# Two decode attentions on one core: all engines' programs rolled into loops over the 16 groups of heads, and a head's maximum taken with a 32x32 transpose on VectorE

## The chip, the core and the metric

The kernel runs on one core of a Trainium2 chip. The metric is the device time of one launch in microseconds (us). TensorE (PE) multiplies matrices, VectorE (DVE) does elementwise work and reductions, ScalarE (ACT) does exponentials and copies, GpSimd (POOL) sets constants, and SyncE (SP) issues nearly all DMA transfers. SBUF holds 128 partitions; PSUM holds the results of matmuls. Each engine runs its own instruction stream and meets the others only at semaphores.

## The reference

The same computation is done twice, for A and for B, with other data. One query token attends to a cache of 8192 keys and values in each of 32 heads of 128 elements; all of it is bf16.

```python
q      = (x @ wq).reshape(1, 1, 32, 128).transpose(0, 2, 1, 3)      # x: 1x1x512, wq: 512x4096
scores = einsum("bhqd,bhkd->bhqk", q, k_cache) * 128 ** -0.5        # k_cache: 1x32x8192x128
p      = softmax(scores, axis=-1)
o      = einsum("bhqk,bhkd->bhqd", p, v_cache)                      # v_cache: 1x32x8192x128
y      = o.transpose(0, 2, 1, 3).reshape(1, 1, 4096) @ wo           # wo: 4096x512
# result: concatenate([y of A, y of B], axis=-1), 1x1x1024
```

Both caches of A and B and the four weights are 285 MB, and each byte is read once.

## The kernel before

**Tiling.** The 64 heads are taken in `NM = 16` groups of `G = 4`; group n is 0 to 7 for A and 8 to 15 for B. A head has 32 partitions, so partition `h*32 + p` holds keys `p*256` to `p*256 + 255` of the group's head h. The keys of a group, called K(n) here, are one transfer of 8192 KB into `kn`, which has two buffers, used in turn; the values V(n) are one transfer of 8192 KB into `vn`, which has one buffer. `vn` first holds both `wq`, and `kn`'s first buffer holds both `wo` at the end.

**A group's work.** K(n) is handled in four chunks c of 64 keys per partition.

- `plan_mul` (L351): DVE multiplies the chunk in place by the broadcast query, 128x8192 elements.
- `plan_red` (L357): PE sums groups of 8 of the 128 products into PSUM `rps`, by 16 matmuls of 512 columns with the identity as weights. Two PSUM slots are used in turn.
- `plan_sr` (L373): DVE sums the last 8, which gives 64 scores per partition in `s_sb`.
- `plan_max` and `plan_gmax` (L379 to L388): DVE takes each partition's maximum `m1`; PE transposes it with an fp32 matmul; DVE takes the maximum of each head's 32 partitions.
- `plan_exp` (L398 to L410): PE spreads the four maxima over the partitions, ACT negates and scales them, and then does four exponentials, one for each head, which also sum.
- `plan_sum` (L415), `plan_pv` (L433): PE sums the sums over partitions, and multiplies the probabilities `pt` with V(n) in 64 matmuls, four at a time in four strips of PSUM `acc`.
- `plan_acc` (L451), `plan_turn` (L459), `plan_o` (L465): ACT copies `acc` out, PE turns it, and DVE divides into `oD`.

**Order.** The values of group n are multiplied a group late. In round n, PE does `red(n,0)`, `red(n,1)`, `red(n,2)`, then `sum(n-1)` and `pv(n-1)`, then `red(n,3)` and `turn(n-1)`. DVE does `mul` 0, 1, `sr` 0, `mul` 2, `sr` 1, `mul` 3, `sr` 2, `sr` 3, the maximum, `o(n-1)`, and the head's maximum. In round 0 there is no `pv`; there the query projection of B, `plan_q(1, 0)` and `plan_q(1, 1)`, stands ahead of `red(0,3)`. The query projection of A stands ahead of all rounds. A `plan_q(a, j)` is 16 matmuls with 32 columns of weights each, four at a time in four strips of `qyp`, and one ACT copy (L339).

**Programs.** `_Plan` records every operation and the waits that it needs, one list for each engine. PE's list is emitted as a loop over rounds 1 to 15 (`_Loop`, `emit_pe`), with one copy of the 16 matmuls for each buffer of `kn` and every address fixed. DVE's is a loop over pairs of rounds. ACT's is written out in full. SP's list is straight code.

**SP's list**, in order: `wq` of A, the two `x`, K(0), `wq` of B, K(1), V(0), K(2), V(1), K(3) and so on to V(14), `wo` of A and half of `wo` of B, V(15) in two pieces, the rest of `wo` of B in five pieces. SP issues one after the other, and each waits as follows:

```python
load_k(n):  red_done[n - 2, 3]      # the buffer's last reduction; K(1) waits only for x
load_v(n):  pv_done[n - 1]          # V(0): q_done[1], the last projection matmul of B
```

**Output projection.** `wo` rows are multiplied with `oD`, spread over partitions (`plan_relayout`, `plan_wo` L528 and L533: four strips at a time); the last 16 heads of B use L572, as their `wo` pieces land.

Of the kernel before, what the change touches and what calls it, by code (L numbers as in the profile page):

```python
# [5 lines left out]
AF = mybir.ActivationFunctionType  # L6
# [6 lines left out]


class _Ctr:


    def __init__(self, nc, stack, name):
        self.sem = stack.enter_context(nc.semaphore(name))
        self.n = 0  # L20
        self.name = name


class _Plan:


    def __init__(self):
        self.prog = {"SP": [], "PE": [], "ACT": [], "DVE": [], "POOL": []}
        self.waited = {}

    def wait(self, eng, mark):
        if mark is None:
            return
        ctr, val = mark
        if val <= 0 or self.waited.get((eng, ctr.name), 0) >= val:
            return
        self.waited[(eng, ctr.name)] = val
        self.prog[eng].append((None, ctr, val))

    def op(self, eng, fn, ctr=None, needs=(), inc=1):  # L40

        for m in needs:
            self.wait(eng, m)
        self.prog[eng].append((fn, ctr, inc))
        if ctr is None:
            return None
        ctr.n += inc
        return ctr, ctr.n


def _emit(e, items, slot=None):
    for fn, ctr, k in items:
        if fn is None:
            e.wait_ge(ctr.sem, k)
        elif isinstance(fn, tuple):
            which, fns = fn
            if slot is None:
                fns[which](e).then_inc(ctr.sem, k)
            else:
                with e.If_eq(slot, 0):  # L60
                    fns[0](e).then_inc(ctr.sem, k)
                with e.Else():
                    fns[1](e).then_inc(ctr.sem, k)
        elif ctr is None:
            fn(e)
        else:
            fn(e).then_inc(ctr.sem, k)


def _steps(items):  # L70


    out, waits = [], []
    for it in items:
        if it[0] is None:
            waits.append(it[1:])
        else:
            out.append((waits, it))
            waits = []
    assert not waits  # L80
    return out


class _Loop:


    def __init__(self, e, rounds):
        self.e = e
        rounds = [_steps(r) for r in rounds]
        assert len({len(r) for r in rounds}) == 1  # L90
        early, self.body, self.last = [], [], []
        for k in range(len(rounds[0])):
            at = [r[k] for r in rounds]
            assert all(it[1:] == at[0][1][1:] for _, it in at)
            first, second, third = at[0][0], at[1][0], at[2][0]
            waits = []
            for (ctr, v), (_, w) in zip(second, third):
                d = w - v
                assert v - d >= 1
                waits.append((ctr, v - d, d))  # L100
            for n, (ws, _) in enumerate(at[1:], 1):
                assert [(c, v) for c, v in ws] == [(c, v + n * d) for c, v, d in waits]
            for ctr, v in first:
                same = [x for c, x, _ in waits if c is ctr]
                if not same:
                    early.append((None, ctr, v))
                else:
                    assert v <= same[0]
            self.body.append((waits, at[0][1]))
            self.last.append([(c, v + len(rounds) * d) for c, v, d in waits])  # L110
        self.early = early
        self.regs = {}
        for k, (waits, _) in enumerate(self.body):
            for i, (ctr, v, d) in enumerate(waits):
                if d:
                    self.regs[k, i] = e.alloc_register("w%d_%d" % (k, i))
                    e.reg_mov(self.regs[k, i], v)

    def emit(self, k, slot):
        e = self.e  # L120
        waits, it = self.body[k]
        for i, (ctr, v, d) in enumerate(waits):
            e.wait_ge(ctr.sem, self.regs.get((k, i), v))
        _emit(e, [it], slot)
        for i, (ctr, v, d) in enumerate(waits):
            if d:
                e.reg_add(self.regs[k, i], self.regs[k, i], d)


def bass_concat_heads__mha_block_cached__gqa_block_cached__decode_kernel(  # L130
# [32 lines left out]
    NK = 2  # L163
# [6 lines left out]
    assert Dh % DW == 0  # L170

    WOG = [[(0, 32)], [(0, 16), (16, 8), (24, 4), (28, 2), (30, 1), (31, 1)]]
    BEFORE = 1
    HT = [32, 16]
    RG = [32, 16, 8, 4, 2]
    VLAST = (0, T - CT, T)

    with ExitStack() as st:
        ec = st.enter_context

        def sb(name, shape, dt):
            return ec(nc.sbuf_tensor(name, shape, dt))

        kn = sb("kn", [P, NK, T, Dh], BF16)
        vn = sb("vn", [P, T, Dh], BF16)

        def flat(ap):
            return ap.rearrange("p t d -> p (t d)")

        W = C * H * Dh  # L190
        assert T * Dh == NA * W
# [37 lines left out]
        def ps(name, shape):  # L229
            return ec(nc.psum_tensor(name, shape, F32))  # L230
# [532 lines left out]
```

## Time and profile before

| what | value |
|---|---|
| time, median of 3 runs | 666.33 us (666.32 to 666.51) |
| the profiled execution's own time | 666.81 us |
| its span, first to last instruction | 665.6 us |
| mean TensorE clock granted | 0.796 |
| PE busy | 377.9 us, 57% |
| DVE busy | 341.2 us, 51% |
| ACT busy | 71.8 us, 11% |
| DMA | 285.31 MB, 429 GB/s over the span |

The times below count from the span's start, so the execution's own time is 1.2 us longer than the span. In a row of the timeline stand start, duration, engine, source line, operation, written tile, read tiles, shape, count, and in brackets how long the engine had been idle and what released it. SPq is SP issuing a transfer. Durations of "x2" and more are from the first start to the last end.

### The profile page before, as it was taken

The numbers are of one execution on the slowest core, as the hardware profiler recorded it, in microseconds if no ns is written. First come the engines' busy times: TensorE is split into PE (matmuls) and PEld (weight loads), VectorE is DVE, ScalarE is ACT, GpSimd is POOL, SyncE is SP. The second block draws the span as 40 slices with busy tenths as digits, with TensorE's granted clock in tenths as the row PEclk, the third lists the DMA queues.
The fourth block names the chain that finished last, engine by engine and source line by source line (L and its number), as shares of the span: only waits on it lengthen the run. The fifth ranks groups of instructions, "written<-read, shape, count | busy, mean of one in ns | idle before, by whom it ended". The sixth has DMA issues, their size and how long they took to land.

```text
span 665.6 us, 6342 instructions
## 1 busy us (share of the span) xinstructions
PE 377.9 (57%) x2569; PEld 176.0 (26%) x2569; DVE 341.2 (51%) x220; ACT 71.8 (11%) x167; POOL 3.0 (0%) x15
## 2 busy tenths in 40 slices
PE   1165755828285582828557281845738184573854
PEld 0022332403132241313224131322413132231422
DVE  1095817456281845638184563818456380835630
ACT  1002020010202011020201002020100202020020
POOL 1000000000000000000000000000000000000000
PEclk9998886959687695968779596877959687795987
DMA  9999999999999999999999999999999999999997
GB/s 380 435 447 434 434 438 437 410 429 441 437 437 437 437 437 418 421 441 441 433 437 437 441 425 410 441 441 433 437 437 441 433 410 433 441 437 433 412 437 302
DMA packets 6069, 285.31 MB, mean 429 GB/s; under 512 B 683, under 2 KB 942, under 8 KB 1198
## 3 DMA queue, kind: packets, MB, share of 16 engines
q1 hardware_dynamic: 6056, 285.22, 99.3%
q8 instruction: 4, 0.07, 0.0%
q14 instruction: 3, 0.02, 0.0%
q10 hardware_dynamic: 6, 0.00, 0.0%
HBM read 285.21 MB, written 0.00 MB: 429 GB/s over the span
## 4 chain that ended last, share of the span: by engine, by line
DMA 40%; PE 29%; DVE 15%; another core or an unknown queue 13%; issue 2%; SPq 0%; DVEq 0%; ACT 0%
PE rps L362 20%; DMA vn<-in_A_v_cache_dram 16%; DVE kn L353 13%; DMA vn<-in_B_v_cache_dram 10%; PE acc L433 8%; DMA kn<-in_A_k_cache_dram 7%; DMA kn<-in_B_wo_dram 5%; DMA kn<-in_B_x_dram 2%; DVE s_sb L373 1%; DVE m L379 1%; PE mtp L385 1%; SPq L256 0%; PE misc L415 0%; ACT xb L317 0%
## 5 line engine op out<-in xcount | busy, mean ns | idle before, releaser
L362 PE MATMUL rps<-kn,ident 128*128 128x512 bf16 x1024 | 265.6, 422 | 242.4 <-DVE kn L353 242.4
L353 DVE TENSOR_TENSOR kn<-kn,qbc 128x8192 bf16<-128x8192 bf16 x64 | 281.5, 4419 | 169.1 <-DMA kn<-in_A_k_cache_dram 89.2
L362 PEld LDWEIGHTS rps<-kn,ident 128*128 128x128 bf16 x1024 | 105.2, 107 | 396.2 <-issue 305.4
L373 DVE TENSOR_REDUCE s_sb<-rps 128x64 f32<-128x512 f32 x64 | 44.0, 688 | 118.0 <-PE rps L362 118.0
L433 PE MATMUL acc<-vn,pt 128*16 128x512 bf16 x1024 | 59.7, 386 | 10.9 <-DMA vn<-in_B_v_cache_dram 10.2
L451 ACT COPY xb<-acc 128x512 f32<-128x512 f32 x16 | 9.4, 585 | 438.6 <-PE acc L433 438.6
L410 ACT ACTIVATE pt<-s_sb,negb 32x256 bf16<-32x256 f32 x64 | 54.8, 857 | 1.9
L433 PEld LDWEIGHTS acc<-vn,pt 128*16 128x16 bf16 x1024 | 24.3, 91 | 39.0 <-DMA vn<-in_B_v_cache_dram 9.6
L398 PE MATMUL bmp<-gm,hrow 1*128 1x1 f32 x128 | 17.8, 256 | 6.0 <-DVE gm L388 6.0
L398 PEld LDWEIGHTS bmp<-gm,hrow 1*128 1x128 f32 x128 | 16.5, 197 | 10.7 <-DVE gm L388 10.0
L459 PEld LDWEIGHTS bmp<-tsel,xb 128*128 128x128 f32 x128 | 16.7, 191 | 3.3 <-ACT xb L451 1.2
L410 ACT ACTIVATION_READ_ACCUMULATOR pt<-s_sb,negb 32x1 f32 x64 | 15.9, 248 | 0.0
L459 PE MATMUL bmp<-tsel,xb 128*128 128x4 f32 x128 | 15.3, 243 | 0.7 <-ACT xb L451 0.7
L402 ACT ACTIVATE negb<-bmp 128x1 f32<-128x1 f32 x16 | 2.7, 171 | 97.1 <-PE bmp L398 97.1
L465 DVE TENSOR_TENSOR oD<-bmp,rinv 128x4 f32 (+1 forms) x16 | 2.4, 153 | 16.6 <-PE bmp L459 16.6
L385 PE MATMUL mtp<-ident_f,m 128*1 128x128 f32 x32 | 6.1, 270 | 8.0 <-DVE m L379 8.0
L313 PE MATMUL misc<-ones_bf,kn 1*128 1x128 bf16 x4 | 0.6, 304 | 13.0 <-DMA kn<-in_B_x_dram 13.0
L388 DVE TENSOR_REDUCE gm<-mtp 1x4 f32<-1x128 f32 x16 | 4.5, 279 | 6.5 <-PE mtp L385 6.5
L331 PE MATMUL qyp<-vn,xb 128*32 128x512 bf16 x64 | 6.0, 504 | 2.2 <-ACT qbc L339 1.5
L379 DVE TENSOR_REDUCE m<-s_sb 128x1 f32<-128x256 f32 x16 | 6.7, 420 | 0.5
L415 PEld LDWEIGHTS misc<-rsum,ones_f 128*128 128x128 f32 x32 | 6.0, 190 | 2.9 <-issue 0.7
L339 ACT CAST qbc<-qyp 128x512 bf16<-128x512 f32 x4 | 2.3, 586 | 38.7 <-PE qyp L331 38.7
(58 smaller groups left out, 39.3 us busy)
## 6 DMA issues: line engine op xcount, KB each, us to landing
vn<-in_B_v_cache_dram SPq DMA_DIRECT2D x1, 6144.0 KB, 24.6
vn<-in_A_wq_dram SPq DMA_DIRECT2D x1, 4096.0 KB, 13.1
vn<-in_B_wq_dram SPq DMA_DIRECT2D x1, 4096.0 KB, 40.6
kn<-in_A_wo_dram SPq DMA_DIRECT2D x1, 4096.0 KB, 41.1
kn<-in_B_wo_dram SPq DMA_DIRECT2D x1, 2048.0 KB, 45.7
vn<-in_B_v_cache_dram SPq DMA_DIRECT2D x1, 2048.0 KB, 29.1
kn<-in_B_wo_dram SPq DMA_DIRECT2D x1, 1024.0 KB, 31.1
kn<-in_B_wo_dram SPq DMA_DIRECT2D x1, 512.0 KB, 31.9
```

Source lines behind the costliest of these rows:

```text
L331: r = e.matmul(qyp[hh * HP:(hh + 1) * HP, :].rearrange("p (i d) -> p i d", d=Dh), xb[:, a, c, hh * HP:(hh + 1) * HP], w, start=(c == 0), s ...
L353: mul_done[n, c] = op("DVE", lambda e: e.tensor_tensor(k, k, qbc[:, nth(n), :].broadcast_to([P, CT, Dh]), ALU.mult), c_mul, [k_in[n], qbc_ ...
L362: r = e.matmul(rps[:, c % 2, :].rearrange("p (t d) -> p t d", d=DW), ident[:], kn[:, i0, c * CT:(c + 1) * CT, i * DW:(i + 1) * DW], start= ...
L373: sr_done[n, c] = op("DVE", lambda e: e.tensor_reduce(s_sb[:, c * CT:(c + 1) * CT], rps[:, c % 2, :].rearrange("p (t d) -> p t d", d=DW), ...
L379: m_done[n] = op("DVE", lambda e: e.tensor_reduce(m1[:], s_sb[:], AX.X, ALU.max), c_dve, [sr_done[n, NCH - 1]])
L385: m = op("PE", lambda e: e.matmul(mtp[0:1, 0:P], m1[:], ident_f[:], start=True, stop=True), c_pe, [m_done[n], i_identf, gm_done.get(n - 1)])
L398: r = e.matmul(bmp[:, 0:1], hrow[0:1, (G - 1 - h) * HP:(G - 1 - h) * HP + P], gm[0:1, h:h + 1], start=(h == 0), stop=(h == G - 1))
L410: p_done[n] = op("ACT", lambda e, h=h, q=q: e.activation(pt[q, :, h], s_sb[q, :], AF.Exp, bias=negb[q, n:n + 1], scale=scale, accum_out=rs ...
L415: m = op("PE", lambda e: e.matmul(misc[:, 0:G], ones_f[:], rsum[:], start=True, stop=True), c_pe, [p_done[n], misc_free[0]])
L433: r = e.matmul(acc[q:q + NT * G, :], pt[:, ts, :].rearrange("p t g -> p (t g)"), vn[:, ts, :].rearrange("p t d -> p (t d)"), start=(j < NP ...
L451: acc_read[n] = op("ACT", lambda e: e.copy(acc_sb, acc[:]), c_act, [pv_done[n], turned.get(n - 1)])
L459: r = e.matmul(bmp[:, NT:NT + G], acc_sb[:, t * Dh:(t + 1) * Dh], tsel[:, t * G:(t + 1) * G], start=(t == 0), stop=(t == NT - 1))
```

## The change

The recording layer is gone, and each engine's program is written as a loop over the groups; addresses in `kn`, `qbc` and `oD` come from registers. PSUM is cut anew: `big` has four banks, two of which take the place of `rps`. Where the order or the waits of the work change:

- **SP** issues the same transfers in the same order. K(n+1) now waits for `mul(n,0)`, the first multiplication of the group before it, and K(2) for all reductions of group 0 and for K(1).
- **PE** does both query projections ahead of all rounds; their matmuls have 128 columns of weights, one at a time, into four PSUM banks, and ACT makes four copies of 32 partitions for each 16. In a round, `red(n,3)` stands ahead of `sum(n-1)` and `pv(n-1)`. The 16 matmuls of a `red` are one and a loop of five times three, with the address computed ahead of each.
- **DVE** takes the head's maximum in one instruction, a reduction that transposes 32x32 blocks, with the result on every partition of the head and negated; PE's transposition and spreading are gone.
- **Output projection:** the 32 and 16 matmuls of a row by `wo` all write one partition, one after the other in loops of four. ACT copies the two rows instead of DVE.

The core of the diff:

```diff
-        def load_k(n):
-            k_in[n] = dma("SP", flat(kn[:, n % NK]), quad(ks, n), s_k[n % NK],
-                          [x_ready if n == KX else red_done.get((n - NK, NCH - 1))])
+        load_wq(1, (s_w, 16))
+        for n in range(NM):
+            if n + 1 < NM:
+                load_k(n + 1, *([(s_red, RED), (s_k, 32)] if n == 1 else [(s_mul, NCH * n + 1)]))
+                load_v(n, (s_pv, n + 1) if n else (s_q, 4 * NA * 2))
...
+        e = nc.tensor
+        with e.Fori(0, NA) as a:
+            e.wait_ge(s_w, rw)
+            e.reg_add(rw, rw, 16)
+            with e.Fori(0, 2) as j:
+                with e.Fori(0, G) as hh:
+                    for c in range(C):
+                        i = e.matmul(
+                            big[:, bass.ds(hh, 1), :].rearrange("p o (i d) -> p (o i) d", d=Dh),
+                            xb[:, a, c, :], wq_v[:, a, c, j, :, hh, :],
+                            start=(c == 0), stop=(c == C - 1))
+                    i.then_inc(s_q, 1)
+                e.wait_ge(s_qc, rq)
+                e.reg_add(rq, rq, G)
...
+        with e.Fori(0, NM + 1) as n:
+            nr = e.alloc_register("pe_nr")
+            e.reg_sub(nr, n1, 1)
+            with e.If_lt(nr, NM):
+                with e.Fori(0, NCH) as c:
+                    e.wait_ge(s_mul, k1)
+                    e.wait_ge(s_sr, k1)
...
+                    e.matmul(o, ident[:], chunk(0), start=True, stop=False, skip_group_check=True)
+                    with e.Fori(0, RL):
+                        for u in range(RU):
+                            i = e.matmul(o, ident[:], chunk((1 + u) * DW), start=False,
+                                         stop=(u == RU - 1), skip_group_check=True)
+                        i.then_inc(s_red, 1)
+                        e.reg_add(ko, ko, RU * DW)
...
+            with e.If_ne(nr, 0):
+                e.wait_ge(s_p, n1)
+                e.matmul(misc[:, 0:G], ones_f[:], rsum[:], start=True, stop=True).then_inc(s_sum, 1)
+                e.wait_ge(s_v, rv)
+                for j in range(T // NT):
...
+        e = nc.vector
+        with e.Fori(0, NM):
+            e.wait_ge(s_k, rk)
...
+            mul(0)
+            mul(1)
+            e.wait_ge(s_p, n1)
+            sr(0)
+            mul(2)
+            sr(1)
+            mul(3)
+            sr(2)
+            sr(3)
+            e.wait_ge(s_sr, ks)
+            e.tensor_reduce(m1[:], s_sb[:], AX.X, ALU.max).then_inc(s_m, 1)
...
+            e.wait_ge(s_turn, n1)
+            e.tensor_tensor(oD_all[:, bass.ds(n * G, G)], tps[:, 0:G], rinv[:],
+                            ALU.mult).then_inc(s_o, 1)
+            e.wait_ge(s_m, n1)
+            e.tensor_reduce(gm[:], m1[:].broadcast_to([P, 32]), AX.X, ALU.max, negate=True,
+                            apply_transpose=True).then_inc(s_gm, 1)
```

PE's program from the query projections to the end of a group's reductions, before; `qyp` takes the projections, `rps` the reductions, and rows 3 and 5 are group 0:

```order
1 L313 MATMUL qyp<-ones_bf,kn 128x128 x4
2 L331 MATMUL qyp<-vn,xb 32x512 x32
3 L362 MATMUL rps<-kn,ident 128x512 x48
4 L331 MATMUL qyp<-vn,xb 32x512 x32
5 L362 MATMUL rps<-kn,ident 128x512 x16
6 L385 MATMUL mtp<-ident_f,m 1x128
7 L398 MATMUL bmp<-gm,hrow 128x1 x4
```

The same stretch after the change, with the waits; `big` takes both, the loop of L219 to L222 runs over A and B and over j, and rows 27 to 38 are a chunk's reduction:

```order
4 L221 REGISTER_ALU [waits s_w]
...
16 L225 MATMUL big<-vn,acc_sb 128x512
...
19 L231 ISA [waits s_qc]
...
23 L259 UNCONDITIONAL_BRANCH [waits c_pool]
...
27 L266 ISA [waits s_sr,s_mul]
28 L268 ISA
29 L268 MATMUL big<-kn,ident 128x512
...
31 L255 ISA
32 L271 MATMUL big<-kn,ident 128x512
...
38 L269 COMPARE_AND_BRANCH
...
76 L318 MATMUL acc<-vn,pt 16x512 [waits s_v]
```

The projection of B, which stood ahead of the last quarter of group 0's reductions, now stands ahead of all of them, behind a wait for `wq` of B (`s_w`) and for ACT's copies (`s_qc`); and `acc`, the product with the values, has moved behind the whole loop of reductions.

SP's program, after the change, from K(0) to V(1):

```order
3 L170 DMA kn<-in_A_k_cache_dram 128x32768
4 L170 DMA vn<-in_B_wq_dram 128x16384 [waits s_w]
5 L170 DMA kn<-in_A_k_cache_dram 128x32768 [waits s_mul]
6 L170 DMA vn<-in_A_v_cache_dram 128x32768 [waits s_q]
7 L170 DMA kn<-in_A_k_cache_dram 128x32768 [waits s_k,s_red]
8 L170 DMA vn<-in_A_v_cache_dram 128x32768 [waits s_pv]
```

The transfers stand as before; what each waits for has moved from ACT's `x` copy (row 5) and from a reduction (row 7 on) to a multiplication and, for K(2), to the reductions of group 0 and the landing of K(1).

More of the change, by code (lines that the diff above doesn't have):

```diff
@@ L12 @@
 P = 128
[L15 to L48, printed above, removed]
@@ L51, in _emit @@
[L51 to L67, printed above, removed]
@@ L70, in _steps @@
[L70 to L127, printed above, removed]
@@ L232, in bass_concat_heads__mha_block_cached__gqa_block_cached__decode_kernel @@
-        rps = ps("rps", [P, 2, 512])
-        acc = ps("acc", [P, 512])
-        mtp = ps("mtp", [P, 512])
-        bmp = ps("bmp", [P, 512])
-        misc = ps("misc", [P, 512])
-        qyp = ps("qyp", [P, 512])
-        yrow = ps("yrow", [P, 512])
-        pl = _Plan()
-        op, wait = pl.op, pl.wait
-        def ctr(name):
-            return _Ctr(nc, st, name)
-        s_x = ctr("s_x")
-        s_w = [ctr("s_w%d" % a) for a in range(NA)]
-        s_wo = [[ctr("s_wo%d%d" % (a, i)) for i in range(len(WOG[a]))] for a in range(NA)]
@@ new lines, in bass_concat_heads__mha_block_cached__gqa_block_cached__decode_kernel @@
+        with e.Fori(0, NA * 2) as j:
+            e.wait_ge(s_q, rq)
+            for hh in range(G):
+                q = slice(hh * HP, (hh + 1) * HP)
+                e.copy(qbc[q, bass.ds(j * 4, 4), :].rearrange("p i d -> p (i d)"),
+                       big[q, hh, :]).then_inc(s_qc, 1)
+            e.reg_add(rq, rq, G)
+        e.wait_ge(c_pool, POOL)
+        with e.Fori(0, NM):
+            e.wait_ge(s_pv, n1)
+            e.copy(acc_sb[:], acc).then_inc(s_acc, 1)
+            e.wait_ge(s_gm, n1)
+            e.activation(negb[:], gm[:], AF.Copy, scale=scale).then_inc(s_nb, 1)
+            e.wait_ge(s_nb, n1)
```

719 lines of the change are left out of this document (281 added, 438 removed).

## The prediction

> **What bounds the kernel now.** I read the page's queue rows first, then SP's waits, then the timeline of the first 130 us.
>
> ```profile
> DMA  9999999999999999999999999999999999999997
> q1 hardware_dynamic: 6056, 285.22, 99.3%
> SPq L256 <- PE acc L433: 515.0, 15, 35.8
> ```
>
> The transfers bound it: the DMA engines are over 90% busy in 39 of 40 slices. SP waits for 515 us in all for `pv` (L433) before it issues the next V, and yet the engines do not pause, since another transfer is queued each time. So an edit on an engine costs nothing as long as each transfer is issued before the one ahead of it lands. The question is where that margin is thinnest. These rows give the pace:
>
> ```profile
> 102.13 8.76 DVE L353 TENSOR_TENSOR kn<-kn,qbc 128x8192 bf16<-128x8192 bf16 x2 [9.88 <-DMA kn<-in_A_k_cache_dram]
> 605.12 8.76 DVE L353 TENSOR_TENSOR kn<-kn,qbc 128x8192 bf16<-128x8192 bf16 x2 [10.21 <-DMA kn<-in_B_k_cache_dram]
> 63.41 8.76 DVE L353 TENSOR_TENSOR kn<-kn,qbc 128x8192 bf16<-128x8192 bf16 x2 [2.80 <-DMA kn<-in_A_k_cache_dram]
> 33.23 8.76 DVE L353 TENSOR_TENSOR kn<-kn,qbc 128x8192 bf16<-128x8192 bf16 x2 [26.74 <-DMA kn<-in_A_k_cache_dram]
> 2.28 0.51 SPq L256 DMA_DIRECT2D vn<-in_B_wq_dram  x1
> vn<-in_B_wq_dram SPq DMA_DIRECT2D x1, 4096.0 KB, 40.6
> 55.20 0.33 SPq L256 DMA_DIRECT2D vn<-in_A_v_cache_dram  x1
> 86.80 34.52 DMA vn<-in_A_v_cache_dram
> ```
>
> From K(2) at 102.1 to K(15) at 605.1 lie 26 transfers, so one takes 19.35 us and a round 38.7. `wq` of B lands at 2.28 + 40.6 = 42.9, K(1) at 63.3, V(0) a transfer later at 82.7, K(2) at 102.0, and V(1), issued at 86.8, at 121.3. V(0) is issued 8 us before K(1) lands, V(1) 15 us before K(2) does.
>
> **The change part by part.** *The settled rounds.* These rows price a round's pieces:
>
> ```profile
> 609.85 9.89 PE L362 MATMUL rps<-kn,ident 128*128 128x512 bf16 x32 [13.84 <-DVE kn L353]
> 37.81 9.19 PE L362 MATMUL rps<-kn,ident 128*128 128x512 bf16 x32 [18.41 <-DVE kn L353]
> 621.65 3.63 PE L362 MATMUL rps<-kn,ident 128*128 128x512 bf16 x16 [1.91 <-DVE kn L353]
> 621.26 0.68 DVE L373 TENSOR_REDUCE s_sb<-rps 128x64 f32<-128x512 f32 x1
> 621.87 4.42 DVE L353 TENSOR_TENSOR kn<-kn,qbc 128x8192 bf16<-128x8192 bf16 x1
> 625.32 3.63 PE L433 MATMUL acc<-vn,pt 128*16 128x512 bf16 x64
> ```
>
> A chunk of 16 matmuls takes 3.63 us. After a pause the first chunk is slower: 32 take 9.19 to 9.89, so the first 16 take 5.6 to 6.3. If mul(n,0) starts at s, then mul 3 ends at s + 20.6 (605.12 to 621.87 + 4.42 is 21.2, and 20.6 with the first chunk at its mean of 5.9). Behind it now come red 3 (0.25 + 3.63), `sum` (0.4) and pv(n-1) (3.63), so V(n) is issued at s + 28.5. In the settled state s is the landing of K(n), and the transfer ahead of V(n) lands at s + 38.7: a margin of 10 us, where before pv stood a chunk earlier. K(n+1) now waits for K(n) to land and be multiplied, s + 4.5, but V(n-1) fills the engines until s + 19.4. Both moves cost nothing there; the cover is gone only if a round's work grows by 10 us.
>
> *The start.* This is where the order of PE bites. Both projections now precede red(0,0), and B's waits until 42.9. Nothing here is hidden from then on. More rows:
>
> ```profile
> 13.68 0.58 ACT L317 CAST xb<-misc 128x512 bf16<-128x512 f32 x1 [5.69 <-PE misc L313]
> 14.16 0.59 ACT L317 CAST xb<-qyp 128x512 bf16<-128x512 f32 x1
> 91.08 0.42 DVE L379 TENSOR_REDUCE m<-s_sb 128x1 f32<-128x256 f32 x1
> 91.41 0.15 DVE L465 TENSOR_TENSOR oD<-bmp,rinv 128x4 f32 x1
> 91.97 0.28 DVE L388 TENSOR_REDUCE gm<-mtp 1x4 f32<-1x128 f32 x1 [0.40 <-PE mtp L385]
> ```
>
> - The first projection of B, 16 matmuls of 512 columns, slow after a pause: 42.9 + 5.9 = 48.8.
> - Four ACT copies, one every 0.48 us, the last taking 0.59, and the handover: 2.2, so 51.0. (L331 had four matmuls at once and one copy. A copy of 32 partitions has as many columns as L317's, so I take that price.)
> - The second: 3.63, to 54.6. V(0) goes out here, as early as before. Four copies: 56.8.
> - red(0,0) with its loop's entry: 0.3 + 3.63, to 60.8. DVE's sr 0 (0.6 to the next), mul 2, sr 1, mul 3: 0.6 + 4.4 + 0.6 + 4.4, to 70.8. red(0,3): 0.25 + 3.63, to 74.7. K(2) goes out here, 8 us before V(0) lands, so no loss yet.
> - sr 3 (0.72 to the next), maximum 0.42, reciprocal and `o` 0.15 each, the head's maximum. No row has a transposing reduction; bounds are 0.15 (`o`) and 0.42 (the longer maximum), and I take 0.28, the row with the nearest role. With 0.1 for each of DVE's waits for itself and 0.3 for the branch back: 2.3, so mul(1,0) starts at 77.0, where before it was 63.4.
> - V(1) is issued 28.5 later, at 105.5.
>
> *Addresses from registers.* The trace has no PE matmul addressed that way; it has DVE's:
>
> ```profile
> 130.30 0.07 DVEq L681
> 130.37 0.22 issue
> 179.40 0.08 DVEq L353
> ```
>
> An address calculation shows as 0.08 and the branch back as 0.07 with 0.22 behind it. Three matmuls of the inner loop need four calculations and one branch. Issuing a matmul costs at most 0.057 (64 in 3.63 us). So PE's sequencer needs 4 x 0.08 + 0.07 + 3 x 0.057 = 0.56, against 3 x 0.227 = 0.68 that the matmuls take: hidden, with some loss at the chunk's start. With 0.22 for each calculation and 0.29 for the branch it is 1.34: a chunk of 6.9. Nearer is the first, since the 0.22 lies behind a branch. I take 0.2 for each of the five chunks on the path, 1.0, and V(1) goes out at 106.5.
>
> The Trainium skill (Advanced Engine Details and Errata, Control Flow Timing) puts a compare-and-branch at about 108 ns; by it the loop of three needs 0.60, an estimate, still under 0.68.
>
> *The gap.* K(2) lands at 102.0, so V(1) is 4.5 us late, and the engines start from empty:
>
> ```profile
> 0.80:1.80 1.00, 0.00 (x0) 0.00 (x0) 0.00 (x0) 0.00 (x0) 0.97 (x5) 1.00 0.00 0
> vn<-in_A_wq_dram SPq DMA_DIRECT2D x1, 4096.0 KB, 13.1
> ```
>
> In the first microsecond after the first issue no byte moves (last columns: DMA share, GB/s). That transfer took 13.1 where half of 19.35 is 9.7: 3.4 more, the two small `x` among it. A restart costs 1.0 to 3.4; I take 1.9, under the middle, since V(1) has no `x` with it. V(1) lands at 106.5 + 1.9 + 19.35 = 127.75, against 121.3: **6.4 us late**. Then the margins return: mul(2,0) starts about 2.5 us after pv(0), at 109; pv(1) ends at 137.5 and V(2) goes out, while K(3) lands at 147. Nothing gives the 6.4 back, for every later byte is queued behind.
>
> *The end.* The chain of waits ends with the last `wo` piece:
>
> ```profile
> 630.79 32.14 DMA kn<-in_B_wo_dram
> 637.28 2.96 PE L533 MATMUL qyp<-kn,o 128*1 128x512 bf16 x32
> 658.74 1.04 PE L433 MATMUL acc<-vn,pt 128*16 128x512 bf16 x16 [0.93 <-DMA vn<-in_B_v_cache_dram]
> ```
>
> L533 ran four at a time (32 in 2.96); now 50 matmuls run singly: 9 slow at 0.43 and 41 at 0.23, 13.3 us from 637.3. With 2.6 for the copy, the spreading and `sum`, and 2.7 for 48 matmuls of pv, PE is ready at 655.9 for the last V piece, used at 658.7: hidden, by 2.8 us. PE's three fewer hops a group, ACT's shorter list and the smaller constants are hidden behind DMA: nothing.
>
> Sum: 665.6 + 6.4 = 672.0 of span. The profiled execution's 666.81 is 0.5 over the median, so from the median: **666.3 + 6.4 = 672.7 us**.
>
> **The rivals.**
>
> *A: one gap at V(1)*, as summed. With no loss to addresses, the two slow chunks at 5.6 and a restart of 1.0, V(1) goes out at 104.9 and it is 3.9 us (670.2); with the two at 6.3, 0.4 for each chunk's addresses and a restart of 3.4, at 108.3 and 9.7 (676.0). Chance 0.64.
>
> *B: PE's sequencer becomes the bound.* At 6.9 us a chunk, red(0,0) and red(0,3) take 3.3 more each, red(0,1), now longer than the 5.0 that DVE's steps hide, 1.9, the projection 0.9: K(2) goes out at 84, after V(0) has landed at 82.7, and lands at 105. Group 1 adds 3.3 + 1.9 + 0.6, V(1) goes out at 121 and is 21 late: 687 or so. For it: 16 calculations stand where none stood. Against it: the 0.08. Anything from 677 on counts here. Chance 0.14.
>
> *C: the gap does not open.* If TensorE stayed fast over its pauses ahead of the first projection of B and of red(1,0), these take 3.63 instead of 5.9, 2.3 less each, and without the 1.0 for addresses V(1) goes out at 101, just ahead of K(2)'s landing: 666.3 to 667.6. Against it: each round's first chunk is slow in this trace. The Trainium skill (TensorE: Matmul & The Clock Gate, Part 1) says so too: it gives about 3.4 us of activity before full rate, and 10 matmuls at 0.43 (4.3 us) agree roughly. Chance 0.10.
>
> *D: faster.* The stream's end is ragged:
>
> ```profile
> 661.00:662.00 1.00, 1.00 (x37) 0.89 (x36) 0.41 (x2) 0.00 (x0) 0.00 (x0) 1.00 0.41 150
> ```
>
> In that microsecond the engines move 150 GB/s and in the next still less, because some finish earlier than others. If V(1) comes just as the last of them finishes K(2), all start it together, the lag is lost and the end comes up to 1.7 us sooner: 664.6. This decides if V(1) is issued between about 100 and 101.5. Chance 0.04.
>
> *E: the single matmuls at the end.* If none of the 50 gets fast, they take 21.4, 8.1 more, of which 2.8 is hidden: pv is 5.3 late, 678 with the gap. Chance 0.06.
>
> *F: code.* The page has `q8` with four instruction transfers, and the kernel before already loops:
>
> ```profile
> q8 instruction: 4, 0.07, 0.0%
> ```
>
> So PE's 15 rounds did not fetch again each time. The Trainium skill (Runtime: NRT & Kernel Launch, Instruction fetch mechanics) warns that a taken branch out of the two loaded blocks stalls for a fetch; by this row that does not happen each round. A stall of one `issue` wait, up to 1 us, at each of three first entries on the path would give 676. Chance 0.02.
>
> **How the numbers follow.** 672.7 is A's. The range takes in A, E, F and the lower half of B, which reaches from 677 to 687, and stops just above C and D: 668.0 to 683.0, with 0.79 in it. A change under 0.2% (1.3 us) cannot be told from none. Faster is D with a little of C, 0.05; the same is C, 0.09; slower is the rest, 0.86.
>
> **What would show it.** Right: mul(1,0) near 77 instead of 63; V(1) issued at 105 to 108, after K(2)'s landing; one slice near 105 us with fewer GB/s; rounds of 38.7 after it; the end unchanged but 6 later. Wrong: warm chunks of over 4.5 us (B), no dip (C or D), idle time of the engines near 655 (E), or a second gap that I have not seen.

## The result, and the profile after

The changed kernel takes **683.63 us** (median of 4 runs, 682.06 to 684.88) against 666.38 us before (4 runs, 666.32 to 666.51): 1.0257 times as long, with an interval of 1.023 to 1.0285. That is 17.3 us slower, where 6.4 were forecast; it lies 0.6 us above the range. The profiled execution took 682.5 us with a span of 681.2, so 15.6 us of span more than before.

The page's DMA slices and queue rows:

```profile
DMA  8999893999999999999999999999999999999997
GB/s 370 439 458 416 350 428 127 431 431 431 431 431 431 431 431 431 431 431 431 431 431 431 431 431 446 443 439 446 431 443 431 431 431 431 431 431 431 408 441 322
q1 hardware_dynamic: 6056, 285.22, 97.1%
q8 instruction: 1, 0.02, 0.0%
```

A slice is 17 us. One of them, from 102 to 119 us, falls to 127 GB/s, and the fifth reads 350; from 119 us on the transfers run unbroken again. So nearly all of the loss lies at the start, as forecast. `q8` and `q14` moved one transfer of code each, where they moved four and three before; that of `q8` falls between 80 and 90 us and that of `q14` behind 640 us, so neither lies in PE's pauses shown below (rival F).

SP's issues in that stretch, from the timeline, are V(0), K(2) and V(1):

```profile
57.73 0.33 SPq L170 DMA_DIRECT2D vn<-in_A_v_cache_dram  x1
82.78 0.33 SPq L170 DMA_DIRECT2D kn<-in_A_k_cache_dram  x1
114.66 0.33 SPq L170 DMA_DIRECT2D vn<-in_A_v_cache_dram  x1
```

The DMA view has the time from each of these issues to its landing, in the same order:

```profile
vn<-in_A_v_cache_dram SPq DMA_DIRECT2D x1, 23.5
kn<-in_A_k_cache_dram SPq DMA_DIRECT2D x1, 23.2
vn<-in_A_v_cache_dram SPq DMA_DIRECT2D x1, 21.8
```

V(0) lands at 81.2 and K(2) goes out 1.6 us after that: a gap that the prediction excluded. K(2) lands at 106.0 and V(1) goes out 8.7 us after that: the gap that it named. V(1) lands at 136.5, 15.2 us later than the 121.3 of before, and K(3)'s multiplication, at 140.8 before, starts as much later. The first row is from before, the others from after the change:

```profile
140.83 8.76 DVE L353 TENSOR_TENSOR kn<-kn,qbc 128x8192 bf16<-128x8192 bf16 x2 [10.35 <-DMA kn<-in_A_k_cache_dram]
73.83 4.42 DVE L403 TENSOR_TENSOR kn<-kn,qbc  x1
82.79 0.69 DVE L408 TENSOR_REDUCE s_sb<-big 128x64 f32<-128x512 f32 x1 [3.07 <-PE big L271]
84.25 0.20 DVE L431 TRANSPOSE_TENSOR_REDUCE gm<-m 128x1 f32<-128x32 f32 x1
84.96 8.76 DVE L403 TENSOR_TENSOR kn<-kn,qbc  x2 [0.51 <-issue]
156.10 8.76 DVE L403 TENSOR_TENSOR kn<-kn,qbc  x2 [7.67 <-DMA kn<-in_A_k_cache_dram]
```

PE's timeline shows why V(1) was so late. The first three rows are B's projection (its second half shows as 4 and 12 matmuls), then the first and the last reduction of group 0, and pv(0). The last two rows are ACT's copies behind the two halves:

```profile
42.95 5.44 PE L225 MATMUL big<-vn,acc_sb 128*128 x16 [12.31 <-DMA vn<-in_B_wq_dram]
51.93 1.02 PE L225 MATMUL big<-vn,acc_sb 128*128 x4 [3.54 <-issue]
53.26 4.44 PE L225 MATMUL big<-vn,acc_sb 128*128 x12 [0.30 <-issue]
62.03 0.61 PE L268 MATMUL big<-kn,ident 128*128 x1 [4.34 <-issue]
62.43 5.74 PE L271 MATMUL big<-kn,ident 128*128 x15
...
78.83 0.38 PE L268 MATMUL big<-kn,ident 128*128 x1
79.05 3.71 PE L271 MATMUL big<-kn,ident 128*128 x15
...
110.98 3.63 PE L318 MATMUL acc<-vn,pt 128*16 128x512 bf16 x64
...
48.52 2.38 ACT L354 CAST qbc<-big 32x512 f32 x4 [15.37 <-PE big L225]
57.83 2.38 ACT L354 CAST qbc<-big 32x512 f32 x4 [6.93 <-PE big L225]
```

The copies end at 50.90 and 60.21, yet PE starts at 51.93 and 62.03. The chain of waits puts the rest down to no wait at all:

```profile
50.91 1.02 issue
60.22 1.81 issue
```

The windows (length, PE busy, granted clock, DMA share, GB/s) show what the pauses did to the 16 matmuls behind each:

```profile
51.90:57.70 5.80, 5.46 (x16) 0.71 0.83 362
62.00:68.20 6.20, 6.17 (x17) 0.58 1.10 476
```

Leaving and entering loops takes 1.02 and 1.81 us of PE's time here (the experiments test this reading), and behind the longer pauses the granted clock was 0.71 and 0.58. The 16 matmuls there took 5.77 and 6.14 us, where the prediction's row for 16 has 3.63. Not all of that excess is the clock: PE also pauses between one round of a loop and the next, 0.30 us in the third row. The delays add up to pv(0), at whose end, 114.6, V(1) goes out.

### The profile page after: what moved, and what is told of

It reads as the page before. It is cut to its first block, busy times and chain, and to the rows that moved or that the text cites. A ratio compares the mean times of both kernels' runs of the same rounds, so it can differ in the third digit from the quotient of the medians.

```text
span 681.2 us, 8028 instructions
## 1 busy us (share of the span) xinstructions
PE 405.4 (60%) x2407; PEld 169.8 (25%) x2407; DVE 338.9 (50%) x218; ACT 80.9 (12%) x182; POOL 2.4 (0%) x13
## 4 chain that ended last, share of the span: by engine, by line
DMA 74%; DVE 12%; PE 10%; issue 2%; ACT 1%; DVEq 0%; ACTq 0%; SPq 0%
DMA kn<-in_B_k_cache_dram 40%; DMA kn<-in_A_k_cache_dram 25%; DVE kn L403 12%; PE big L271 6%; DMA vn<-in_B_wq_dram 4%; DMA vn<-in_B_v_cache_dram 3%; DMA vn<-in_A_wq_dram 2%; PE big L225 2%; PE acc L318 1%; PE big L268 1%; ACT qbc L354 1%; PE tps L324 0%; PE yrow L243 0%; DVEq L398 0%; DVE s_sb L408 0%
## 5 line engine op out<-in xcount | busy, mean ns | idle before, releaser
L403 DVE TENSOR_TENSOR kn<-kn,qbc x64 | 281.5, 4419 | 123.6 <-DMA kn<-in_B_k_cache_dram 57.7
L271 PE MATMUL big<-kn,ident 128*128 x960 | 272.9, 432 | 0.0
L268 PE MATMUL big<-kn,ident 128*128 x64 | 28.2, 441 | 216.7 <-DVE kn L403 212.4
L271 PEld LDWEIGHTS big<-kn,ident 128*128 128x128 bf16 x960 | 103.3, 108 | 154.2 <-issue 100.3
L408 DVE TENSOR_REDUCE s_sb<-big 128x64 f32<-128x512 f32 x64 | 44.1, 689 | 115.1 <-PE big L271 115.1
L360 ACT COPY acc_sb<-acc 128x512 f32<-128x512 f32 x16 | 9.4, 586 | 479.0 <-PE acc L318 478.9
L268 PEld LDWEIGHTS big<-kn,ident 128*128 128x128 bf16 x64 | 6.3, 98 | 233.9 <-issue 231.8
L225 PE MATMUL big<-vn,acc_sb 128*128 x64 | 21.5, 505 | 21.8 <-DMA vn<-in_B_wq_dram 12.3
L324 PE MATMUL tps<-tsel,acc_sb 128*128 128x4 f32 x128 | 17.7, 261 | 11.0 <-ACT acc_sb L360 10.4
L324 PEld LDWEIGHTS tps<-tsel,acc_sb 128*128 128x128 f32 x128 | 16.3, 199 | 19.1 <-ACT acc_sb L360 17.9
L354 ACT CAST qbc<-big 32x512 f32 x16 | 9.2, 577 | 36.0 <-PE big L225 35.7
L293 PE MATMUL big<-kn,o 128*1 x48 | 12.4, 421 | 0.0
```

The lines of the kernel that those rows point to most:

```text
L225: i = e.matmul(big[:, bass.ds(hh, 1), :].rearrange("p o (i d) -> p (o i) d", d=Dh), xb[:, a, c, :], wq_v[:, a, c, j, :, hh, :], start=(c = ...
L268: e.matmul(o, ident[:], chunk(0), start=True, stop=False, skip_group_check=True)
L271: i = e.matmul(o, ident[:], chunk((1 + u) * DW), start=False, stop=(u == RU - 1), skip_group_check=True)
L293: i = e.matmul(y, o2[:, bass.ds(h + u, 1)], wo_sb[:, h + u, :], start=False, stop=False, skip_group_check=True)
L324: i = e.matmul(tps[:, 0:G], acc_sb[:, t * Dh:(t + 1) * Dh], tsel[:, t * G:(t + 1) * G], start=(t == 0), stop=(t == NT - 1))
L354: e.copy(qbc[q, bass.ds(j * 4, 4), :].rearrange("p i d -> p (i d)"), big[q, hh, :]).then_inc(s_qc, 1)
```

## The experiments

Theory T: B's two projection halves, now ahead of `red(0,0)` with a copy behind each, put pauses into PE's path, and TensorE loses its clock in them; V(1) goes out too late. The rivals: PE's loops with register addresses are slower everywhere; the moved pv does it; the new maximum does it; SP's new waits or the new end do it.

**The order and the shape of the projection.** First, the changed kernel with B's projection put back inside group 0, ahead of `red(0,2)` and `red(0,3)`, in banks of its own and written out without loops:

```diff
-        with e.Fori(0, NA) as a:
+        with e.Fori(0, 1) as a:
...
+                    with e.If_eq(k1, 3):
+                        e.wait_ge(s_w, 32)
+                        proj_b(0)
+                    with e.If_eq(k1, 4):
+                        e.wait_ge(s_qc, 3 * G)
+                        proj_b(1)
```

> The changed kernel with one thing undone: the two halves of B's query projection stand ahead of the third and the fourth chunk of group 0 again (their shape, 16 single matmuls and four ACT copies each, is kept; they get PSUM banks of their own). Theory 'order at the start' (the 17 us are two empty stretches of the transfer queue, because group 0's reductions wait for B's weights): reductions of group 0 start near 38 us instead of 62, the first multiplication of group 1 near 67 instead of 85, V(1) is issued near 96, before K(2) lands; time 666 to 668. Rival 'slower loops' (PE loses time in every round to addresses and branches): 680 or more, since no loop is changed.

Measured: 667.9 us (666.24 to 669.22), ratio 1.0023 [1.0013, 1.0034]. In its timeline V(1) goes out ahead of K(2)'s landing, and no stretch is empty:

```profile
94.24 0.33 SPq L170 DMA_DIRECT2D vn<-in_A_v_cache_dram  x1
```

Second, the order kept, but the projections in the shape of before (32 columns of weights, four strips, one copy for each half), written out without loops, and with two banks, so that PE does not wait between the halves:

```diff
-        with e.Fori(0, NA) as a:
...
+        for a in range(NA):
...
-                            big[:, bass.ds(hh, 1), :].rearrange("p o (i d) -> p (o i) d", d=Dh),
-                            xb[:, a, c, :], wq_v[:, a, c, j, :, hh, :],
+                            big[hh * HP:(hh + 1) * HP, 2 + j, :].rearrange("p (i d) -> p i d", d=Dh),
+                            xb[:, a, c, hh * HP:(hh + 1) * HP], wq_v[:, a, c, j, :, hh, :],
...
-            for hh in range(G):
...
+            e.copy(qbc[:, j * 4:(j + 1) * 4, :].rearrange("p i d -> p (i d)"),
+                   big[:, 2 + j % 2, :]).then_inc(s_qc, 1)
```

> The changed kernel with the projections' shape undone and their order kept: 16 matmuls of 32 columns in four strips at a time, fixed addresses, two PSUM banks of their own and one ACT copy for each half, so that the reductions need not wait for the copies. Theory 'order at the start': order alone costs little, what hurts is how long the projection of B and its handovers hold PE. Both halves take about 4 us from 42.9, reductions start near 47 (62 in the changed kernel), group 1's first multiplication near 70, V(1) near 99, K(2) lands at 101 to 102: no gap or one under 2 us, 665 to 668. If the place ahead of the reductions is itself the cause, whatever the shape, V(1) stays near 110 and the time near 680.

Measured: 667.23 us (666.14 to 668.88), 1.0016 [1.0006, 1.0026]. PE and SP in its timeline:

```profile
42.06 3.64 PE L226 MATMUL big<-vn,acc_sb 128*32 128x512 bf16 x32 [23.80 <-DMA vn<-in_B_wq_dram]
45.63 0.61 PE L267 MATMUL big<-kn,ident 128*128 x1
64.50 0.33 SPq L170 DMA_DIRECT2D kn<-in_A_k_cache_dram  x1
95.42 0.33 SPq L170 DMA_DIRECT2D vn<-in_A_v_cache_dram  x1
```

Both halves take 3.64 us together and PE goes straight on. V(1) goes out at 95.42, 19 us sooner. Both kernels keep the loops over groups and the reductions with their register addresses, SP's new waits, the late pv, the new maximum and the new end, and 15.7 and 16.4 of the 17.3 us are gone. So the loss arises at B's projection, and the rivals by which loops are slower everywhere, or SP's waits or the end do it, fall. Both also write out B's projection without loops, so they do not part its place and shape from its loops; later runs do.

**Keeping TensorE busy.** In the changed kernel, 12 matmuls of the identity into an unused bank behind each half fill the wait for the copies; work is only added:

```diff
+                for _ in range(12):
+                    e.matmul(yrow, ident[:], ident[:, None, :].broadcast_to([P, NQ, P]),
+                             start=True, stop=True)
                 e.wait_ge(s_qc, rq)
```

> The changed kernel with twelve matmuls of 512 columns added, into an unused bank and read by nobody, behind each half of a projection, while ACT copies. Theory 'TensorE slows down in the handovers': the pauses of 3.5 and 4.3 us between the halves and before group 0 shrink to 1 to 1.5 us, the second half takes 3.6 to 4 instead of 5.8, and the first reduction of group 0 3.6 to 4 instead of 6.1; V(0) goes out 2 us sooner, group 1 starts 4 to 5 us sooner, the first empty stretch closes, and the time falls to 674 to 679 though work was added. Rival 'the sequencer sets the pace there': the added matmuls cost their own time, 5 us, and the time is 684 to 690.

Measured: 680.27 us (680.14 to 682.5), 1.0208 [1.0191, 1.0225]: faster though work was added, but less than expected, and with a range that overlaps the changed kernel's by 0.4 us. Its timeline:

```profile
52.82 1.02 PE L226 MATMUL big<-vn,acc_sb 128*128 x4 [1.00 <-issue]
54.12 1.02 PE L226 MATMUL big<-vn,acc_sb 128*128 x4 [0.27 <-issue]
...
62.08 0.39 PE L272 MATMUL big<-kn,ident 128*128 x1 [1.72 <-issue]
62.33 3.95 PE L275 MATMUL big<-kn,ident 128*128 x15
```

`red(0,0)` is fast now, 4.20 us instead of 6.14, and the second half takes 4.95 instead of 5.77. The pauses of 1.00 and 1.72 for the loops stay, and between each four matmuls 0.27 to 0.30: added matmuls cannot hide those. So of the 2.14 and 2.51 us that the two pieces took over 3.63 in the changed kernel, the clock has 0.8 and 1.9, and the loops with their register addresses 1.3 and 0.6. V(1) went out at 112.84, 1.8 us sooner, in the slowest of the four executions.

**The late pv.** The changed kernel with `sum` and pv ahead of the last chunk, as before:

```diff
-                with e.Fori(0, NCH) as c:
+                with e.Fori(0, NCH - 1) as c:
...
                 i.then_inc(s_pv, 1)
+            with e.If_lt(nr, NM):
+                e.wait_ge(s_mul, k1)
+                e.wait_ge(s_sr, k1)
+                ...
```

> The changed kernel with the product of the group before and the values put ahead of the last chunk of a group's reductions again, as before the change. Theory 'order at the start': V(1) goes out one chunk earlier, 4 us, and every later byte with it: 678 to 681 (a wide interval, since the changed kernel itself runs from 682 to 685). In the settled rounds nothing moves, for there the transfer ahead covers it. If the product's place did matter in each round, 15 rounds of 4 us would give far more than 4.

Measured: 678.65 us (677.28 to 679.62), 1.0189 [1.0172, 1.0206]; V(1) went out at 109.70, 5.0 us sooner, and the time is 5.0 less. So it is part of the size, not the cause.

**Register addresses.** The 16 matmuls of a reduction written out, with fixed addresses for each buffer:

```diff
-                    with e.Fori(0, RL):
-                        for u in range(RU):
-                            i = e.matmul(o, ident[:], chunk((1 + u) * DW), start=False,
...
+                    with e.If_eq(ko, 0):
+                        reds(0, c)
+                    with e.Else():
+                        reds(1, c)
```

> The changed kernel with the reductions written out with fixed addresses, one copy for each buffer of kn, as before the change (the loops over groups, the projections, the order and all else kept). Theory 'order at the start': addresses from registers cost about 0.6 us for a chunk at full TensorE clock and nothing for a slow one (the run with added matmuls showed 4.2 for a chunk at full clock, 3.63 before the change); four or five chunks lie on the way to V(1), so 680 to 683, at most 3 us under the changed kernel. Rival 'slower loops': most of the 17 us go, 672 or less.

Measured: 682.25 us (680.77 to 682.99), 1.0234 [1.0218, 1.025], 1.4 us less in the median, with intervals that overlap; V(1) went out no sooner (114.99). Rival B, PE's sequencer as the bound of the reductions, is out.

**The kernel before with the new projection alone.** No loop and no address changes; only the order and the shape of B's projection:

```diff
+        for j in range(QA // 4):
+            plan_q(1, j)
+        wait("PE", qy_free[0])
         for n in range(NM):
...
-                            qyp[hh * HP:(hh + 1) * HP, :].rearrange("p (i d) -> p i d", d=Dh),
-                            xb[:, a, c, hh * HP:(hh + 1) * HP], w,
+                        r = e.matmul(qb[hh][:].rearrange("p (i d) -> p i d", d=Dh),
+                                     xb[:, a, c, :], w, start=(c == 0), stop=(c == C - 1))
```

> The kernel before with one part of the change alone: both projections ahead of all groups, in 128-column weights, into four PSUM banks, with four ACT copies each, all written out with fixed addresses; product of values ahead of the last chunk, as before. By the prediction's own working (pauses of 2.2 us, full clock behind them) V(1) goes out near 101, just as K(2) lands: 666 to 667.5. If TensorE's clock falls in these pauses too, without any loop, the second half and the first chunks are slow, V(1) goes out at 103 to 105 and the time is 669 to 672. If loops and branches have no part at all in the changed kernel's pauses, pauses of 3.5 and 4.3 appear here as well and V(1) is near 107: 673 to 676.

Measured: 670.88 us (670.51 to 672.4), 1.0073 [1.0057, 1.0088]: the order and the shape cost 4.5 us by themselves, with straight code and the early pv. The pauses of straight code are shorter:

```profile
51.73 1.89 PE L333 MATMUL qyp<-vn,xb 128*128 128x512 bf16 x4 [2.47 <-ACT qbc L341]
59.49 6.86 PE L364 MATMUL rps<-kn,ident 128*128 128x512 bf16 x31 [2.47 <-ACT qbc L341]
102.66 0.33 SPq L256 DMA_DIRECT2D vn<-in_A_v_cache_dram  x1
```

2.47 us each, where the prediction took 2.2, against 3.54 and 4.34 with the loops. After the first, matmuls were slow (1.89 for four), after the second they were not.

**The maximum.** The kernel before with the transposing reduction alone:

```diff
-            m = op("PE", lambda e: e.matmul(mtp[0:1, 0:P], m1[:], ident_f[:],
-                                            start=True, stop=True), c_pe,
...
+                gm[:], m1[:].broadcast_to([P, 32]), AX.X, ALU.max, negate=True,
+                apply_transpose=True), c_dve, [m_done[n], nb_done.get(n - 1)])
```

> The kernel before with the other part of the change alone: the head's maximum by one transposing reduction on VectorE, negated, read by ACT; PE's transposition and spreading are gone. Theory: it shortens a chain that the transfers cover in every round, 666.1 to 666.6, no difference; between the end of the row maximum and the first exponential it should save about 1.5 us in each round, which shows only in the trace. If that chain were on the path, 15 rounds of 1.5 would show as 20 us.

Measured: 666.37 us (666.21 to 666.41), 0.9999 [0.999, 1.0009]: no difference. The instruction takes 0.21 us there, and the first exponential starts 0.93 us after `m` instead of 2.51, but nothing waits for it.

**The projection's loops.** The changed kernel with PE's projections written out with fixed addresses, order and shape kept; then the same with 11 matmuls of the identity behind each half:

```diff
-        with e.Fori(0, NA) as a:
-            with e.Fori(0, 2) as j:
-                with e.Fori(0, G) as hh:
+        for a in range(NA):
+            for j in range(2):
+                for hh in range(G):
```

> The changed kernel with PE's projections written out with fixed addresses instead of three nested loops; shape, copies, order and all other loops kept. The kernel before with the new projection showed pauses of 2.47 us where the changed kernel has 3.54 and 4.34. Theory 'the loops stretch the pauses': the pause between the halves falls to 2.5, that ahead of group 0 to 3 to 3.6 (the entry of the loop over groups stays), V(0) goes out 1 to 1.5 us sooner and V(1) 1.5 to 4 sooner, as the first chunk of group 0 is still slow or no longer so: 678 to 682. If loops have no part in it, 683 to 684 as the changed kernel.

> The same, with eleven added matmuls of 512 columns behind each half (2.5 us, the time of the copies). This makes the two assumptions of the prediction's sum true: pauses of about 2.2 to 2.5 and TensorE at full clock behind them. If the sum failed by these two alone, the start is as it said: second half 3.6, reductions of group 0 from about 57, group 1 at 77 to 79, V(1) at 106 to 109, one empty stretch, 672 to 676. If it stays at 679 or more, a third term is wrong.

Measured: 678.68 us (678.35 to 679.1), 1.0182 [1.0166, 1.0198], and 676.38 us (674.79 to 677.04), 1.0141 [1.0126, 1.0157], the second 0.4 us above what was expected. The timelines of the one and the other:

```profile
50.02 3.63 PE L224 MATMUL big<-vn,acc_sb 128*128 128x512 bf16 x16 [2.57 <-ACT qbc L351]
57.58 0.60 PE L265 MATMUL big<-kn,ident 128*128 x1 [3.93 <-issue]
57.98 5.68 PE L268 MATMUL big<-kn,ident 128*128 x15
```

```profile
50.49 3.63 PE L225 MATMUL big<-vn,acc_sb 128*128 128x512 bf16 x16 [0.20 <-ACT qbc L355]
58.12 0.39 PE L269 MATMUL big<-kn,ident 128*128 x1 [1.63 <-issue]
58.36 3.98 PE L272 MATMUL big<-kn,ident 128*128 x15
108.18 0.33 SPq L170 DMA_DIRECT2D vn<-in_A_v_cache_dram  x1
```

Without the projection's loops the second half is fast, after a pause of 2.57; `red(0,0)`, after 3.93, is not. With TensorE busy both are, and the second half ends at 54.1, V(1) goes out at 108.2: the prediction's 54.6 and 106.5, nearly. From V(1)'s issue to the end of the time it is still 2.0 us more than the prediction had (568.2 for 566.2).

**The end, and a version without the loss.** The kernel with the strips still varied from 666.1 to 668.9, and in its profiled execution the last V piece met slow matmuls. Twelve, then four matmuls of the identity ahead of that piece (the lines show twelve):

```diff
+                            for _ in range(12):
+                                e.matmul(big[:, 0, :], ident[:],
+                                         ident[:, None, :].broadcast_to([P, NQ, P]),
+                                         start=True, stop=True)
                             e.wait_ge(s_v1, 16)
```

> The changed kernel with the projections in strips (as in the run with strips) and twelve added matmuls of 512 columns into an unused bank while PE waits for the last quarter of V(15). Theory: in the run with strips the loss left is at the end, where TensorE is slow after its wait (1.91 for 16 matmuls of pv, 1.87 for the turn, 1.0 for rows that took 0.6); kept busy it is fast, the end falls back on the last transfer, which there lands about 0.7 us sooner than in the kernel before: 665.3 to 666.3, level with before or just under it. If the end's chain is long for another reason, 667 as in the run with strips.

> The changed kernel with the projections in strips and four added matmuls (0.9 us) instead of twelve ahead of the last quarter of V(15). Twelve came too late where the quarters before had been slow (they ended at 660.3, the values were there at 658). With four the last quarter waits at most 0.5 us, and TensorE is less often slow behind it: 665.6 to 666.8. If it still spreads from 666 to 669, the end is slow for a reason that these matmuls do not touch.

Measured: 667.26 us (666.16 to 668.9), 1.0013 [1.0004, 1.0022], a miss; and 666.33 us (666.05 to 667.36), 0.9999 [0.999, 1.0008], level with the kernel before (666.43). The rows of twelve, and of four:

```profile
653.20 4.45 PE L321 MATMUL acc<-vn,pt 128*16 128x512 bf16 x48 [0.97 <-DMA vn<-in_B_v_cache_dram]
660.28 1.04 PE L321 MATMUL acc<-vn,pt 128*16 128x512 bf16 x16
```

```profile
656.04 1.04 PE L315 MATMUL big<-ident 128*128 128x512 bf16 x4
658.14 1.04 PE L321 MATMUL acc<-vn,pt 128*16 128x512 bf16 x16 [1.06 <-DMA vn<-in_B_v_cache_dram]
```

With twelve, the 48 matmuls ahead were slow themselves, and the added ones ran until 660.3, past the piece's landing near 658: they cost what they should have saved. Four end at 657.1. No version beat the kernel before: the transfers bound both.

## Why the prediction was wrong in size

**Right: the place and the mechanism.** V(1) goes out after K(2) has landed, the engines stand empty, and nothing gives the time back. Over the seven kernels with this gap, the time follows V(1)'s issue:

| kernel | V(1) issued | time | difference |
|---|---|---|---|
| before, new projection | 102.66 | 670.88 | 568.2 |
| written out, TensorE busy | 108.18 | 676.38 | 568.2 |
| pv early | 109.70 | 678.65 | 569.0 |
| projection written out | 110.14 | 678.68 | 568.5 |
| TensorE busy | 112.84 | 680.27 | 567.4 |
| the change | 114.66 | 683.63 | 569.0 |
| fixed addresses | 114.99 | 682.25 | 567.3 |

The issues span 12 us and the differences 1.7. The issue is that of the one profiled execution and the time a median; with the profiled executions' own times the differences run from 567.4 to 569.7.

**Wrong: the two handovers and the two pieces of PE work behind them**, in the bullets of "The start". The prediction took 2.2, 3.63, 2.2 + 0.3 and 3.63, in all 12.0 us. Measured: 3.54, 5.77, 4.34 and 6.14, in all 19.8. These 7.8 are nearly all of the 8.0 by which mul(1,0) was late, 84.96 against 77.0. The prediction had the right row, that the first chunk after a pause is slow, and used it ahead of B and of `red(1,0)`, but took full speed behind the two pauses that its own sum had just opened. And it priced the projection's loops at nothing, and the entry of the reductions' loop at 0.3, where leaving and entering loops took 1.02 and 1.81 and the gaps inside them more. By the run with TensorE kept busy, the 7.8 part into about 4.4 for the loops and register addresses (1.02, 1.81 less 0.3, 1.3 and 0.6), 2.8 for the clock and 0.6 for the copies, which with their handovers took 2.5 instead of 2.2. Rival F had a price near that of the loops, for another cause, code fetches, of which the trace shows none in the two pauses.

**The other terms.** The first half took 5.44 for 5.9. DVE's steps from `red(0,0)` to mul 3's end took 10.1 for 10.0, and `red(0,3)` 4.5 for 3.9. From `red(0,3)` to mul(1,0) it was 2.2 for 2.3, the new maximum in it 0.20 for 0.28. From mul(1,0) to V(1) it was 29.7, for 28.5 and what of the 1.0 for addresses lies in group 1; by its own rows the prediction's 20.6 to the end of mul 3 is 20.8 (21.2 less 0.36), so 0.2 of this is a slip in its sum. A chunk with register addresses at full clock took 4.20 and 4.22 in the two busy kernels, 0.6 over the 3.63; 0.2 was taken. Most chunks on the path were slow from the clock, which left little of this to gain: 1.4 us in the medians. The restart of V(1) cost 21.8 - 19.35 = 2.45, for 1.9.

**"K(2) goes out here, 8 us before V(0) lands, so no loss yet"** failed with the same 8 us. Yet this second gap has no price of its own: V(1) waits for pv(0), whose start depends on mul(1,0) and not on K(2). Two of the kernels above show it: with pv early and with the projection written out, V(1) goes out 0.4 us apart, K(2) 4.7 us apart (83.04 and 78.31), and the times are 678.65 and 678.68.

**The sum.** Of the 10.9 us between 672.7 and 683.63, V(1)'s landing gives 8.7 (136.5 for 127.75), and the tail from the last V piece to the end 0.5 (7.35 for 6.86, with PE's slower rows below). The other 1.6 is how the two profiled executions stand to their medians, the one 1.1 under, the other 0.5 over.

```profile
662.62 3.62 PE L293 MATMUL big<-kn,o 128*1 x16
673.85 1.08 PE L318 MATMUL acc<-vn,pt 128*16 128x512 bf16 x16 [2.34 <-DMA vn<-in_B_v_cache_dram]
675.61 1.87 PE L324 MATMUL tps<-tsel,acc_sb 128*128 128x4 f32 x8 [0.68 <-ACT acc_sb L377]
```

**The rivals.** A came true in kind; its upper end, 676.0, took the slow chunks at 6.3 but still only two of them. B's times, from 677 on, hold the measured one, but its cause was not there: the fixed addresses gave 1.4 us. C needed TensorE to stay fast, and it was slower than even A had it. D's condition, V(1) between 100 and 101.5, did not come about. E falls: the last 16 single matmuls ran fast (3.62) and ended before the last piece landed. That the order and shape of the projection cost 4.5 us, its loops 5.0 and the late pv 5.0 is measured by one edit each, the first from the kernel before, the others from the changed one; they need not add up, and 2.8 us are left for the addresses and for what these do to each other.

**Open.** Why the changed kernel's four runs lie in two pairs (682.1 and 682.5, 684.8 and 684.9) was not settled. The start or the end of TensorE's slow stretches could do it; no run shows it.

## What to carry to other kernels

In a kernel bound by transfers, find the one place where an issue has the least margin, and walk the chain to it step by step: here a projection moved ahead of the first reduction, with a few us more of PE's time, cost most of 17 us. For every wait that a sum puts into TensorE's path, add it up with slow matmuls behind it as well as with fast ones: in the rows shown here waits of 2.0 to 2.6 us were followed by either, those of 3.5 us and more by matmuls that were slow at least in part. A loop that is left or entered there needs a price too. Once the start was mended (the kernel with strips and four added matmuls), rolled loops and register addresses cost nothing that could be measured, since each settled round has some 10 us to spare.

## What the runs showed of the hardware

**Short pauses already cost TensorE its clock, sometimes.** A pause of 2.04 us ahead of a chunk gave a granted clock of 0.57 in the changed kernel and of 1.00 in the one with strips (from the windows; the first row has PE's columns alone, the second those of all engines):

```profile
101.00:105.00 4.00, 3.82 (x10) 0.57 0.61 262
```

```profile
55.40:59.50 4.10, 4.10 (x16) 1.50 (x16) 4.10 (x2) 0.00 (x0) 0.00 (x0) 1.00 1.18 512
```

Those of 2.47 went either way too, in one kernel; those of 3.54, 3.93 and 4.34 were all followed by slow matmuls. The fall can also come late: behind the pause of 3.54 in the changed kernel the first four matmuls took 1.02 us at a granted clock of 1.00, and the next twelve 4.44 us at 0.62. The Trainium skill (TensorE: Matmul & The Clock Gate, Part 1) gives an idle window of about 3.4 us for the fall, by a window that runs freely. The longer pauses agree; the slow chunks after 2.04 and 2.47 come sooner than that figure.

**Leaving and entering nested loops costs PE 0.9 to 1.8 us** behind a wait. In the changed kernel it was 0.89 behind the landing of `wq` of B (42.06 to 42.95), 1.02 and 1.81 behind the copies; with TensorE busy 1.07 and 1.79 behind the copies. Written out, the projection started 0.14 behind the landing, and the second pause had 1.42 and 1.49, for entering the loops of the rounds and the reductions alone. The kernel before with the new projection, in straight code there, started `red(0,0)` 0.06 behind the last copy. The Trainium skill (Advanced Engine Details and Errata, Control Flow Timing) has 108 ns for a compare-and-branch; eight to seventeen of these would be needed, an estimate from these pauses, and the traces do not show what else the time went into.

**A transfer of 8192 KB into empty engines takes longer, by 2.3 to 3.9 us**: V(1) took 21.8 to 22.2 from issue to landing in the seven kernels with the gap, and K(2), where it too went out after V(0) had landed, 21.6 (pv early), 21.9 (fixed addresses) and 23.2 (the change), against 19.35 in a full queue.
